# Weights as fp32 over the hardware rings with casts on chip, shared taps and diagonals, and half rows of x, in a fused convolution and GELU block

## The chip, the cores and the metric

The kernel runs on one core of one Trainium2 chip. Its matrix products run on TensorE (PE in the profiles); VectorE (DVE), ScalarE (ACT) and GpSimd (POOL) do the element-wise work; SyncE (SP) only issues transfers here. A "ring" is the queue of transfers of an engine. The metric is the device time of one execution in microseconds (us); lower is better. Each kernel was run several times beside the kernel before on the same chip. Beside each run stands the mean clock that TensorE was granted (1.00 is full speed).

## The reference, cut to what matters

```python
w = softmax(weight, axis=-1)                 # 8 heads x 7 taps
x_pad = concat([zeros(B, 6, 192), x], 1)     # causal, 8 x 4096 x 192
y[b, s, ch] = sum_k w[head(ch), k] * x_pad[b, s + k, ch]     # head(ch) = ch // 24
h = y.reshape(32768, 192) @ w_in             # 192 x 2048
out = gelu(h) @ w_out                        # 2048 x 192, fp32 out
```

All inputs and the output are fp32 in memory; the two matrix products run in bf16.

## The kernel before

The 32768 tokens are cut into two halves that run side by side in partitions 0 to 63 and 64 to 127, and each half into blocks: six of 256 tokens, then blocks of 512. Blocks 0 and 1 are convolved by TensorE with diagonal matrices (the taps), the later ones by VectorE. Per block TensorE does the first product in slices, ScalarE applies gelu to each slice, and TensorE does the second product of the block before between the slices.

The weights come over GpSimd's queue, whose DMAs cast fp32 to bf16 on the way. Half of `win` is loaded, and VectorE copies each piece across to the other 64 partitions (`dup`):

```python
for i in range(3):                      # GpSimd
    win_in(FP[i], FP[i + 1], S_WIN[i])  # win (bf16) <- moe_w_in (fp32), two halves
halo(0)
g.dma_start(ap(wout, ...), ap(woutt, ...)).then_inc(S_WOUT, 16)   # patterns cut
# ... cut ...
v.tensor_scalar(wnm[0:H, 0:KS], wex[:, :], wrc[:, 0:1], None, ALU.mult)   # VectorE: softmax,
v.transpose(wnt[:, :], wnm[:, :])       # then a column of taps per channel, by transposes
for q in range(4):
    v.transpose(ap(wcol, 32 * q * NP * 32, ...), ap(wch, DQ * (q % 2), ...))
diag(0); diag(1)                        # diagonals of two thirds; ScalarE makes the third's
for p in range(NP): trans(0, p)         # x of block 0, in whole rows: 32x32 transposes
dup(0)
conv_out(v, 0, 1); conv_out(v, 0, 4)    # convolved block 0 out of PSUM
dup(1); dup(2)
for p in range(NP): trans(1, p)
for p in range(NP): cast(1, p)
for j in range(len(PIECES)): conv_out(v, 1, j)
# ... cut: then transposes and convolution of block 2 and on ...
t.wait_ge(S_WARM, 1)                    # TensorE
for i in range(16):
    t.matmul(hp[1][:, 0:512], warm[:, 0:128], warm[:, :])   # warm-ups on zeros
```

In block 0, gelu groups 0 to 7 need the weight slices in pairs: groups 0 and 1 need slice 0, groups 4 and 5 need slice 2. The second product of block 0 is spread over block 1's eight groups as 3, 4, 4, 4, 4, 4, 4, 4 parts of 31 (6 units of 64 in the first).

## Time and profile before

| | before |
|---|---|
| median of three runs | 683.74 us (683.59 to 684.27) |
| span of the profiled run | 682.0 us |
| first tap on TensorE | 7.51 us |
| first gelu | 10.59 us |
| first second-product matmul | 19.24 us |
| first first-product matmul of block 2 | 29.76 us |

The last four lines are read from the instructions in order of time and from the chain of work that ended last. They are the marks by which kernels are compared: once the second product has begun, TensorE hardly waits any more, so whatever is lost or won up to there is carried to the end.

### The profile page before, as it was taken

The page shows a single profiled execution, that of the slowest core. Times are in us where ns is not written, and L with a number is a line of the kernel's source. Part 1 is how long each engine was busy: PE and PEld are TensorE (multiplying, and loading weights), DVE is VectorE, ACT ScalarE, POOL GpSimd, SP SyncE. Part 2 cuts the span into 40 slices and gives each one's busy share as a digit, 9 for nine tenths or more (in the row PEclk, how much of TensorE's full clock was granted, in tenths as well). Part 3 has the DMA queues.
Part 4 walks back from the last instruction along what each step waited for, and adds up shares of the span by engine and source line. Part 5 has one row for each costly group of instructions (what it writes and reads, how often), then busy time and mean ns, then how long its engine had stood idle before and what let it go on. Part 6 is the DMA issues. An engine that isn't in the chain of part 4 may idle for free.

```text
span 682.0 us, 27319 instructions
## 1 busy us (share of the span) xinstructions
PE 676.2 (99%) x12576; PEld 407.5 (60%) x12576; DVE 562.2 (82%) x909; ACT 538.4 (79%) x557; POOL 35.1 (5%) x51
## 2 busy tenths in 40 slices
PE   8999999999999999999999999999999999999998
PEld 4899655555555555555555555555555555555556
DVE  7899979888889888899888898888898888988611
ACT  7899988777787777787777788777778777778772
POOL 4026100000000000000000000000000000000000
PEclk9999999999999999999999999999999999999999
DMA  9345322134432143332234322334422434310223
GB/s 178 77 107 130 83 60 72 44 78 95 95 94 54 45 94 94 95 77 52 63 94 95 94 68 45 80 94 96 94 53 46 95 94 96 82 43 21 48 49 94
DMA packets 132946, 54.00 MB, mean 79 GB/s; under 512 B 126432, under 2 KB 132704, under 8 KB 132832
## 3 DMA queue, kind: packets, MB, share of 16 engines
q1 hardware_dynamic: 129872, 49.93, 31.5%
q0 software_dynamic: 2288, 1.57, 1.6%
q8 instruction: 98, 1.61, 1.0%
q10 hardware_dynamic: 672, 0.76, 0.4%
q14 instruction: 16, 0.13, 0.1%
HBM read 28.66 MB, written 25.17 MB: 79 GB/s over the span
## 4 chain that ended last, share of the span: by engine, by line
PE 97%; ACT 2%; issue 0%; DVE 0%
PE hp L774 47%; PE ob L838 43%; PE ob L805 6%; ACT gT L694 2%; PE hp L708 1%; PE ob L727 0%; ACT xc L192 0%; ACT osb L261 0%; DVE osb L303 0%; DVE osb L272 0%; DVE warm L452 0%
## 5 line engine op out<-in xcount | busy, mean ns | idle before, releaser
L694 ACT ACTIVATE gT<-hp 128x1024 bf16<-128x1024 f32 x512 | 522.8, 1023 | 129.3 <-PE hp L774 126.0
L774 PE MATMUL hp<-xc,win 64*64 64x512 bf16 (+2 forms) x6048 | 418.9, 366 | 1.5 <-ACT gT L694 0.7
L838 PE MATMUL ob<-gT,wout 64*64 64x512 bf16 x5376 | 366.3, 376 | 0.0
L561 DVE SCALAR_TENSOR_TENSOR acc<-xT,wcol,acc 128x512 f32<-128x512 f32 (+1 forms) x495 | 314.6, 700 | 0.5 <-ACT acc L667 0.5
L774 PEld LDWEIGHTS hp<-xc,win 64*64 64x64 bf16 (+1 forms) x6048 | 187.7, 106 | 136.3 <-ACT gT L694 2.5
L838 PEld LDWEIGHTS ob<-gT,wout 64*64 64x64 bf16 x5376 | 172.2, 118 | 122.9
L303 DVE STREAM_TRANSPOSE osb<-ob 128x512 f32<-128x512 f32 x84 | 74.2, 886 | 100.8 <-PE ob L838 100.8
L528 DVE STREAM_TRANSPOSE xT<-xin 128x512 f32<-128x512 f32 (+1 forms) x105 | 78.7, 803 | 2.1 <-DMA xin<-in_x_dram 2.1
L561 DVE SCALAR_TENSOR_TENSOR xc<-xT,wcol,acc 128x512 bf16<-128x512 f32 (+1 forms) x99 | 65.3, 717 | 0.0
L438 POOL COPY xT<-xT 128x18 f32<-128x18 f32 x30 | 27.9, 930 | 515.3 <-DVE xT L528 492.3
L805 PE MATMUL ob<-wout,gT 64*128 64x192 bf16 x1024 | 52.2, 243 | 0.3
L805 PEld LDWEIGHTS ob<-wout,gT 64*128 64x128 bf16 x1024 | 43.5, 94 | 6.4 <-PE ob L805 0.6
L554 DVE TENSOR_SCALAR acc<-xT,wcol 128x512 f32<-128x512 f32 (+1 forms) x90 | 37.6, 474 | 1.1
L274 ACT ACTIVATE osb<-ob 128x192 f32<-128x192 f32 x4 | 1.3, 330 | 9.5 <-PE ob L805 9.5
L272 DVE COPY osb<-ob 128x192 f32<-128x192 f32 x4 | 1.4, 357 | 8.4 <-PE ob L805 8.4
L708 PE MATMUL hp<-warm 128*128 128x512 bf16 x16 | 6.3, 581 | 1.3 <-DVE warm L452 1.3
L261 ACT ACTIVATE osb<-ob 128x384 f32<-128x384 f32 x12 | 5.8, 487 | 0.0
L667 ACT ACTIVATE acc<-xT,wcol 128x256 f32<-128x256 f32 (+1 forms) x9 | 5.2, 575 | 0.0
L708 PEld LDWEIGHTS hp<-warm 128*128 128x128 bf16 x16 | 2.1, 139 | 4.9 <-issue 3.6
L194 DVE CAST xc<-ob 64x256 bf16<-64x256 f32 (+3 forms) x8 | 2.8, 358 | 1.6 <-PE ob L727 1.4
L376 POOL DMA_DIRECT2D win<-in_moe_w_in_dram x6 | 3.9, 653 | 0.0
L497 DVE COPY win<-win 64x768 bf16<-64x768 bf16 (+1 forms) x6 | 3.1, 509 | 0.2
(33 smaller groups left out, 21.7 us busy)
## 6 DMA issues: line engine op xcount, KB each, us to landing
out_dram<-osb SPq DMA_DIRECT2D x122, 192.0 KB, 3.1
xin<-in_x_dram SPq DMA_DIRECT2D x116, 192.0 KB, 4.1
xin<-in_x_dram SPq DMA_DIRECT2D x20, 96.0 KB, 3.2
wout<-in_moe_w_out_dram POOLq DMA_DIRECT2D x1, 768.0 KB, 11.0
win<-in_moe_w_in_dram POOLq DMA_DIRECT2D x4, 96.0 KB, 4.2
win<-in_moe_w_in_dram POOLq DMA_DIRECT2D x2, 192.0 KB, 4.8
out_dram<-osb SPq DMA_DIRECT2D x8, 48.0 KB, 1.7
out_dram<-osb ACTq DMA_DIRECT2D x4, 96.0 KB, 1.9
```

Of the source, the lines that this page charges most:

```text
L261: e.activation(out=dst, in_=src, func=AF.Copy).then_inc(S_EVA)
L303: v.transpose(ap(osb[m % 2], j, [[8 * C, 128], [C // 2, TB // 32], [NP, 32]]), bank(ring(m, j)),).then_inc(S_EV)
L438: g.tensor_copy(dst, src).then_inc(S_HALO)
L528: v.transpose(ap(xT[n % 2], p * XW + HX, [[NP * XW, 128], [1, w]]), ap(xin[n % NX], p, [[TB // 32 * DQ, 128], [D if n == 0 else DQ, w // 3 ...
L554: ins = v.tensor_scalar(a, src, wk, None, ALU.mult)
L561: ins = v.scalar_tensor_tensor(dst, src, wk, a, op0=ALU.mult, op1=ALU.add)
L667: a.activation(out=acc[n % 2][:, p * TB : p * TB + w], in_=ap(xT[n % 2], p * XW + HX, [[NP * XW, 128], [1, w]]), func=AF.Copy, scale=wcol[ ...
L694: a.activation(out=ap(gT[n % 2], i * c * 2 * w, dst), in_=ap(hp[u % 2], 0, src), func=AF.Gelu,).then_inc(S_GELU)
L708: t.matmul(hp[1][:, 0:512], warm[:, 0:128], warm[:, :])
L774: ins = t.matmul(hp[u % 2][fo : fo + fw, o : o + w], ap(win, f1, [[NP * F, 64], [2, fw]]), xc[n % 2][r, p * TB : p * TB + w], start=(p == ...
L805: ins = t.matmul(bank(bb[sub], w=C), gT[m % 2][r, c0 : c0 + 128], wout[r, CH[i] * C : (CH[i] + 1) * C], start=(ph == 0 and i == 0), stop=( ...
L838: ins = t.matmul(bank(ring(m, j), slice(64 * h, 64 * h + 64), w), ap(wout, 64 * hf * NF * C + CH[i] * C + j, [[NF * C, 64], [NP, 64]],), g ...
```

## The change

The intent is a shorter start: take the weights off GpSimd's slower queue, shorten the chain that makes the taps, load less of x first, and spread the casts over two engines. The whole weights are now loaded as fp32 by SyncE and ScalarE and cast by VectorE and GpSimd: `own` casts a piece of `win` where it landed, `dup` casts it across to the other half of the partitions, and `wcast` casts a piece of `wout`. The diff, cut to its core:

```diff
-        wcol = sbt("wcol", [128, NP * 32], F32)
-        dg = sbt("dg", [128, NP * KS * 64], BF16)
+        wcol = sbt("wcol", [128, KS], F32)
+        winf = sbt("winf", [128, NP * F // 2], F32)
+        woutf = sbt("woutf", [128, NF * C], F32)
+        dg = sbt("dg", [128, KS * 64], BF16)
 ... GpSimd
+            g.dma_start(wsb[:, :], ap(wt, 0, [[KS, H], [0, 64 // H], [1, KS]])).then_inc(S_WSB, 16)
 ...
-            for i in range(3):
-                win_in(FP[i], FP[i + 1], S_WIN[i])
             halo(0)
-            g.dma_start(ap(wout, ...), ap(woutt, ...)).then_inc(S_WOUT, 16)
+            own(g, OWNG[0]).then_inc(S_OWN)          # cast of weight slice 1
             halo(1)
+            for p in range(NP):
+                cast(1, p)                           # block 1's x to bf16
+            own(g, OWNG[1]).then_inc(S_OWN)          # cast of weight slice 3
+            for i in range(2):
+                wcast(g, i).then_inc(S_WOG)          # half of wout
 ... VectorE
-            diag(0)
-            diag(1)
             for p in range(NP):
                 trans(0, p)
-            dup(0)
+            own(v, 0).then_inc(S_DUPE)               # cast of weight slice 0
+            dup(0, 0)                                # reads winf (fp32), writes win (bf16)
             conv_out(v, 0, 1)
             conv_out(v, 0, 4)
-            dup(1)
-            dup(2)
+            dup(0, 1)
+            dup(1, 0)
+            dup(1, 1)
             for p in range(NP):
                 trans(1, p)
-            for p in range(NP):
-                cast(1, p)
+            own(v, 2).then_inc(S_DUPE)
+            for s in (2, 3):
+                for hf in range(2):
+                    dup(s, hf)
             for j in range(len(PIECES)):
                 conv_out(v, 1, j)
+            for i in range(2, 4):
+                wcast(v, i).then_inc(S_WOC)          # the other half of wout
 ... ScalarE
             load(a, 0, (2, 3))
             a.wait_ge(S_PRO, 1)
             a.activation(out=wex[:, :], in_=wsb[:, :], func=AF.Exp, ...)
+            for s in range(2):
+                win_in(a, s, 1)
 ... TensorE
-            share = {1: [3, 4, 4, 4, 4, 4, 4, 4]}
 ... SyncE
-            sp.dma_start(wsb[:, :], ap(wt, 0, [[KS, H], [1, KS]])).then_inc(S_WSB, 16)
             load(sp, 0, (0, 1))
-            sp.wait_ge(S_WIN[0], 32)
+            for s in range(2):
+                win_in(sp, s, 0)
             load(sp, 1)
+            for s in range(2, 4):
+                for hf in range(2):
+                    win_in(sp, s, hf)
+            for i in range(4):
+                wout_in(sp, i)
             load(sp, 2)
```

More of the change, by code (lines that the diff above doesn't have):

```diff
@@ L112, in bass_lightweight_conv__then__act_gelu_exact_kernel @@
         wout = sbt("wout", [128, NF * C], BF16)
-        wsb = sbt("wsb", [H, KS], F32)
-        wmx = sbt("wmx", [H, 1], F32)
-        wsm = sbt("wsm", [H, 1], F32)
-        wrc = sbt("wrc", [H, 1], F32)
-        wex = sbt("wex", [H, KS], F32)
-        wnm = sbt("wnm", [32, 32], F32)
-        wnt = sbt("wnt", [32, 32], F32)
-        wch = sbt("wch", [32, D], F32)
-        wcol = sbt("wcol", [128, NP * 32], F32)
+        wsb = sbt("wsb", [64, KS], F32)
+        wmx = sbt("wmx", [64, 1], F32)
+        wsm = sbt("wsm", [64, 1], F32)
+        wrc = sbt("wrc", [64, 1], F32)
+        wex = sbt("wex", [64, KS], F32)
+        wcol = sbt("wcol", [128, KS], F32)
+        winf = sbt("winf", [128, NP * F // 2], F32)
+        woutf = sbt("woutf", [128, NF * C], F32)
         idb = sbt("idb", [128, 64], BF16)
-        dg = sbt("dg", [128, NP * KS * 64], BF16)
+        dg = sbt("dg", [128, KS * 64], BF16)
         warm = sbt("warm", [128, 512], BF16)
@@ L136, in bass_lightweight_conv__then__act_gelu_exact_kernel @@
         S_WSB = sem("S_WSB")
-        S_WIN = [sem("S_WIN%d" % i) for i in range(3)]
-        S_WOUT = sem("S_WOUT")
+        S_WIN = [sem("S_WIN%d" % i) for i in range(4)]
+        S_WOUT = [sem("S_WOUT%d" % i) for i in range(4)]
         S_XIN = [sem("S_XIN%d" % i) for i in range(NX)]
@@ L151, in bass_lightweight_conv__then__act_gelu_exact_kernel @@
         S_PCA = sem("S_PCA")
-        S_DGA = sem("S_DGA")
         S_DUPE = sem("S_DUPE")
+        S_OWN = sem("S_OWN")
+        S_WOC = sem("S_WOC")
+        S_WOG = sem("S_WOG")
         S_HALO = sem("S_HALO")
@@ L203, in wait_pc, with cast, own, wcast @@
                 e.wait_ge(S_PCE, 2 + (1, 3, 6)[p])
+        def cast(e, n, p):
+            e.wait_ge(S_TR, NP * n + p + 1)
+            e.tensor_copy(
+                ap(xTb[PC[n]], p * XB + HX, [[NP * XB, 128], [1, WS[n]]]),
+                ap(xT[n % 2], p * XW + HX, [[NP * XW, 128], [1, WS[n]]]),
+            ).then_inc(S_CAST[PC[n]])
         NCV = NP * KS
-        FQ = F // 8
         FH = F // 2
-        FP = [0, FQ, 2 * FQ, FH]
+        FP = [0, 256, 512, 768, FH]
+        OWNV = (0, 2)
+        OWNG = (1, 3)
+        WG = [0, 4, 2, 6]
+        def own(e, s):
+            e.wait_ge(S_WIN[s], 32)
+            return e.tensor_copy(
+                ap(win, FP[s], [[NP * F, 128], [F, NP], [1, FP[s + 1] - FP[s]]]),
+                ap(winf, FP[s], [[NP * FH, 128], [FH, NP], [1, FP[s + 1] - FP[s]]]),
+            )
+        def wcast(e, i):
+            e.wait_ge(S_WOUT[i], 16)
+            o = 2 * WG[i] * C
+            return e.tensor_copy(wout[:, o : o + 4 * C], woutf[:, o : o + 4 * C])
+        def win_in(e, s, hf):
+            e.dma_start(
+                ap(winf, 64 * hf * NP * FH + FP[s], [[NP * FH, 64], [FH, NP], [1, FP[s + 1] - FP[s]]]),
+                ap(wint, hf * FH + FP[s], [[NP * F, 64], [F, NP], [1, FP[s + 1] - FP[s]]]),
+            ).then_inc(S_WIN[s], 16)
+        def wout_in(e, i):
+            g = WG[i]
+            e.dma_start(
+                ap(woutf, 2 * g * C, [[NF * C, 128], [2 * C, 2], [1, 2 * C]]),
+                ap(woutt, 256 * g * C, [[2 * C, 128], [256 * C, 2], [1, 2 * C]]),
+            ).then_inc(S_WOUT[i], 16)
         def cvd(n):
@@ L313, in load @@
                 off = ((q // 2) * HALF + OFF[n]) * D + DQ * (q % 2)
+                dst = [[TB // 32 * DQ, 32], [DQ, mb], [1, DQ]]
                 if n == 0:
-                    dst = [[TB // 32 * DQ, 32], [1, mb * D - DQ]]
-                    src = [[mb * D, 32], [1, mb * D - DQ]]
+                    src = [[mb * D, 32], [D, mb], [1, DQ]]
                 else:
-                    dst = [[TB // 32 * DQ, 32], [DQ, mb], [1, DQ]]
                     src = [[D, 32], [32 * D, mb], [1, DQ]]
@@ L373, in _ @@
         def _(g):
-            def win_in(c0, c1, sm):
-                for hf in range(2):
-                    g.dma_start(
-                        ap(win, 64 * hf * NP * F + c0, [[NP * F, 64], [F, NP], [1, c1 - c0]]),
-                        ap(wint, hf * FH + c0, [[NP * F, 64], [F, NP], [1, c1 - c0]]),
-                    ).then_inc(sm, 16)
+            g.dma_start(
+                wsb[:, :], ap(wt, 0, [[KS, H], [0, 64 // H], [1, KS]])
+            ).then_inc(S_WSB, 16)
             g.wait_ge(S_MSET, 1)
@@ L441, in _ @@
             halo(0)
-            g.dma_start(
-                ap(wout, 0, [[NF * C, 128], [2 * C, NF // 2], [1, 2 * C]]),
-                ap(woutt, 0, [[2 * C, 128], [256 * C, NF // 2], [1, 2 * C]]),
-            ).then_inc(S_WOUT, 16)
+            own(g, OWNG[0]).then_inc(S_OWN)
             halo(1)
+            for p in range(NP):
+                cast(g, 1, p)
+            own(g, OWNG[1]).then_inc(S_OWN)
+            for i in range(2):
+                wcast(g, i).then_inc(S_WOG)
             for n in range(2, NB):
@@ L453, in _ @@
             v.memset(idb[:, :], 1.0).then_inc(S_MSET)
-            v.memset(wnm[:, :], 0.0).then_inc(S_MSET)
             v.wait_ge(S_WSB, 16)
@@ L463, in _ @@
             v.wait_ge(S_PRO, 3)
-            v.wait_ge(S_MSET, 2)
-            v.tensor_scalar(
-                wnm[0:H, 0:KS], wex[:, :], wrc[:, 0:1], None, ALU.mult
-            ).then_inc(S_PRO)
-            v.wait_ge(S_PRO, 4)
-            v.transpose(wnt[:, :], wnm[:, :]).then_inc(S_PRO)
-            v.wait_ge(S_PRO, 5)
-            v.tensor_copy(
-                ap(wch, 0, [[D, 32], [GRP, H], [1, GRP]]),
-                ap(wnt, 0, [[32, 32], [1, H], [0, GRP]]),
-            ).then_inc(S_PRO)
@@ L476, in _ @@
-            v.wait_ge(S_PRO, 6)
-            for q in range(4):
-                v.transpose(
-                    ap(wcol, 32 * q * NP * 32, [[NP * 32, 32], [1, NP * 32]]),
-                    ap(wch, DQ * (q % 2), [[D, 32], [1, NP], [NP, 32]]),
-                ).then_inc(S_PRO)
-            v.wait_ge(S_PRO, 10)
-            v.wait_ge(S_IDN, 2)
-            def diag(p):
-                v.tensor_tensor(
-                    ap(dg, p * KS * 64, [[NP * KS * 64, 128], [64, KS], [1, 64]]),
-                    ap(idb, 0, [[64, 128], [0, KS], [1, 64]]),
-                    ap(wcol, p * 32, [[NP * 32, 128], [1, KS], [0, 64]]),
-                    ALU.mult,
-                ).then_inc(S_DG)
@@ L493, in dup @@
-            def dup(s):
-                v.wait_ge(S_WIN[s], 32)
-                for hf in range(2):
-                    v.tensor_copy(
-                        ap(
-                            win,
-                            64 * (1 - hf) * NP * F + FH + FP[s],
-                            [[NP * F, 64], [F, NP], [1, FP[s + 1] - FP[s]]],
-                        ),
-                        ap(
-                            win,
-                            64 * hf * NP * F + FP[s],
-                            [[NP * F, 64], [F, NP], [1, FP[s + 1] - FP[s]]],
-                        ),
-                    ).then_inc(S_DUPE)
@@ L510, in cast @@
-            def cast(n, p):
-                v.wait_ge(S_TR, NP * n + p + 1)
-                v.tensor_copy(
-                    ap(xTb[PC[n]], p * XB + HX, [[NP * XB, 128], [1, WS[n]]]),
-                    ap(xT[n % 2], p * XW + HX, [[NP * XW, 128], [1, WS[n]]]),
-                ).then_inc(S_CAST[PC[n]])
+            for hf in range(2):
+                v.tensor_scalar(
+                    wcol[64 * hf : 64 * hf + 64, :], wex[:, :], wrc[:, 0:1], None, ALU.mult
+                ).then_inc(S_PRO)
@@ new lines, in _, with dup @@
+            v.wait_ge(S_PRO, 5)
+            v.wait_ge(S_IDN, 2)
+            v.tensor_tensor(
+                ap(dg, 0, [[KS * 64, 128], [64, KS], [1, 64]]),
+                ap(idb, 0, [[64, 128], [0, KS], [1, 64]]),
+                ap(wcol, 0, [[KS, 128], [1, KS], [0, 64]]),
+                ALU.mult,
+            ).then_inc(S_DG)
+            def dup(s, hf):
+                v.wait_ge(S_WIN[s], 32)
+                v.tensor_copy(
+                    ap(
+                        win,
+                        64 * (1 - hf) * NP * F + FH + FP[s],
+                        [[NP * F, 64], [F, NP], [1, FP[s + 1] - FP[s]]],
+                    ),
+                    ap(
+                        winf,
+                        64 * hf * NP * FH + FP[s],
+                        [[NP * FH, 64], [FH, NP], [1, FP[s + 1] - FP[s]]],
+                    ),
+                ).then_inc(S_DUPE)
@@ L532, in trans @@
                         p,
-                        [[TB // 32 * DQ, 128], [D if n == 0 else DQ, w // 32], [NP, 32]],
+                        [[TB // 32 * DQ, 128], [DQ, w // 32], [NP, 32]],
                     ),
@@ L550, in conv @@
                 src = ap(xT[n % 2], p * XW + HF + kt, [[NP * XW, 128], [1, w]])
-                wk = wcol[:, p * 32 + kt : p * 32 + kt + 1]
+                wk = wcol[:, kt : kt + 1]
                 a = acc[n % 2][:, p * TB : p * TB + w]
@@ L616, in _ @@
         def _(a):
-            a.wait_ge(S_WARM, 1)
-            a.activation(out=hot[:, 0:1], in_=warm[0:1, 0:1], func=AF.Exp).then_inc(S_ACTP)
+            a.activation(
+                out=hot[:, 0:1], in_=nc.const_aps.tensor(0.0, (1, 1), F32), func=AF.Exp
+            ).then_inc(S_ACTP)
             load(a, 0, (2, 3))
@@ L628, in _ @@
             ).then_inc(S_ACTP)
-            a.activation(out=hot[:, 1:2], in_=warm[0:1, 0:1], func=AF.Gelu).then_inc(S_HOT)
-            a.wait_ge(S_PRO, 10)
-            a.wait_ge(S_IDN, 2)
-            for k in range(KS):
-                d0 = ((NP - 1) * KS + k) * 64
-                c0 = (NP - 1) * 32 + k
-                a.activation(
-                    out=dg[:, d0 : d0 + 64],
-                    in_=idb[:, :],
-                    func=AF.Copy,
-                    scale=wcol[:, c0 : c0 + 1],
-                ).then_inc(S_DGA)
+            a.activation(
+                out=hot[:, 1:2], in_=nc.const_aps.tensor(0.0, (1, 1), F32), func=AF.Gelu
+            ).then_inc(S_HOT)
+            for s in range(2):
+                win_in(a, s, 1)
+            a.wait_ge(S_PRO, 5)
             for p in range(NP):
@@ L670, in first_tap @@
                     func=AF.Copy,
-                    scale=wcol[:, p * 32 + KS - 1 : p * 32 + KS],
+                    scale=wcol[:, KS - 1 : KS],
                 ).then_inc(S_K0)
@@ L715, in pconv @@
                     if n == 0:
-                        if p < NP - 1:
-                            t.wait_ge(S_DG, p + 1)
-                        else:
-                            t.wait_ge(S_DGA, KS)
+                        t.wait_ge(S_DG, 1)
                 if k == KS - 2:
@@ L724, in pconv @@
                     r = slice(64 * hf, 64 * hf + 64)
-                    d0 = (p * KS + k) * 64
+                    d0 = k * 64
                     x0 = p * XB + (32 * k if n == 0 else HF + k) + c0
@@ L759, in mm1 @@
                         t.wait_ge(S_CV, cvd(n))
-                if n == 0 and i in (0, 2, 4):
-                    t.wait_ge(S_WIN[i // 2], 32)
-                    t.wait_ge(S_DUPE, 2 * (i // 2) + 2)
+                if n == 0:
+                    t.wait_ge(S_DUPE, (2, 3, 4, 5, 7, 8, 9, 10)[i])
+                    t.wait_ge(S_OWN, sum(s <= i // 2 for s in OWNG))
                 for cc in range(c):
@@ L869, in _ @@
                     new = M0 < n <= M1
-                    ws = SHARE if new else share.get(n, [1] * NSL[n])
+                    ws = SHARE if new else [1] * NSL[n]
                     a0 = len(todo) * sum(ws[:i]) // sum(ws)
                     a1 = len(todo) * sum(ws[: i + 1]) // sum(ws)
-                    if n == 1 and a0 == 0 and a1 > 0:
-                        t.wait_ge(S_WOUT, 16)
+                    if n == 1 and i < 2:
+                        t.wait_ge((S_WOG, S_WOC)[i], 2)
                     for un in todo[a0:a1]:
@@ L885, in _ @@
         def _(sp):
-            sp.dma_start(wsb[:, :], ap(wt, 0, [[KS, H], [1, KS]])).then_inc(S_WSB, 16)
             load(sp, 0, (0, 1))
-            sp.wait_ge(S_WIN[0], 32)
+            for s in range(2):
+                win_in(sp, s, 0)
             load(sp, 1)
+            for s in range(2, 4):
+                for hf in range(2):
+                    win_in(sp, s, hf)
+            for i in range(4):
+                wout_in(sp, i)
             load(sp, 2)
-            sp.wait_ge(S_WOUT, 16)
             load(sp, 3)
```

## The prediction

> **What bounds the kernel now.** I read the page's busy table and its chain of work that ended last, then the same chain for the first 20 us, then the start in order of time, and last the waits, because the change touches only the start.
>
> ```profile
> PE 676.2 (99%) x12576; PEld 407.5 (60%) x12576; DVE 562.2 (82%) x909; ACT 538.4 (79%) x557; POOL 35.1 (5%) x51
> PE 97%; ACT 2%; issue 0%; DVE 0%
> ```
>
> TensorE holds 97% of the chain. Every byte of weights and both prologue blocks are over by about 20 us, so the other 660 us cannot change except by being shifted. What counts is the moment at which TensorE begins its unbroken run. The chain of the first 20 us, piece by piece (start, length, what):
>
> ```profile
> 1.26 6.32 PE hp L708 x16
> 7.58 0.90 PE ob L727 x22
> 8.50 0.38 ACT xc L192
> ...
> 9.94 0.63 PE hp L774 x8
> 10.59 1.94 ACT gT L694 x2
> ...
> 13.62 0.83 PE hp L774 x12
> 14.45 0.89 PE ob L727 x28
> ...
> 18.51 0.83 PE hp L774 x12
> 19.34 0.58 PE ob L805 x12
> ```
>
> L708 is the 16 warm-up matmuls, L727 the convolution taps of blocks 0 and 1, L192 the ScalarE copies of the convolved block, L774 the first matmul, L694 gelu, L805 the second matmul. The reader is to see that the chain does not pass through the x load, the softmax of the taps or the diagonals. It passes through the warm-ups, which end at 7.58, and the taps follow at once. From 10.59 to about 18.5 it alternates between gelu and TensorE; from 18.51 it is TensorE without a gap.
>
> The same stretch in order of time (start, us, engine, line), and then its waits (who waited for whom: us in total, times, longest):
>
> ```profile
> 6.36 1.34 DVE L528 STREAM_TRANSPOSE xT<-xin 128x256 f32<-128x256 f32 x3
> ...
> 7.51 1.63 PE L727 MATMUL ob<-xTb,dg 64*64 64x256 bf16 x56
> ...
> 19.39 1.34 DVE L528 STREAM_TRANSPOSE xT<-xin 128x256 f32<-128x256 f32 x3 [1.72 <-DMA xin<-in_x_dram]
> ```
>
> ```profile
> PEld ob L727 <- ACT xTb L643: 0.4, 1, 0.4
> ...
> PEld ob L727 <- DVE xTb L512: 0.2, 1, 0.2
> ...
> PEld ob L805 <- DMA wout<-in_moe_w_out_dram: 0.2, 1, 0.2
> ```
>
> The first two lines show that TensorE takes its first tap at 7.51, before the modelled end of the last warm-up, and that the transposes of block 0 start at 6.36, after the diagonals. The third of them is block 2's transposes, which waited 1.72 us for x. The waits are of weight loads that stood ready 0.4, 0.2 and 0.2 us early; the matmuls in front of them covered most of that. So the waits that the change can remove are small.
>
> **What the Trainium skill says.** "TensorE: Matmul & The Clock Gate", Part 1, says that an idle array runs at half rate until a window of activity has passed, with 426.7 ns between 512-column matmuls. This trace agrees: the warm-up weight loads stand 0.43 us apart (1.66, 2.09, ... 5.93, 6.36), tighter only at the last ones. "DMA: Bandwidth & Descriptors", SWDGE vs HWDGE vs iDMA, says that only DMAs issued by GpSimd can cast; so fp32 over the hardware rings needs casts on the engines. The trace fits: both weights are issued by POOL. "VectorE: DVE Perf Modes", The perf-mode tier table, gives an fp32 copy in SBUF the two-fold rate; here the cast of 128x256 fp32 to bf16 took 285 ns, less than the 350 ns of the one-pass scaling of the same shape and less than the 424 ns out of PSUM. "SBUF — State Buffer", SBUF: two separate sides, says that VectorE in such a mode and GpSimd shut each other out of a shared port pair. The trace shows something of that kind: POOL's 18-element copy took about 300 ns in the first 34 us and 1001 ns after, beside a busy VectorE.
>
> **The change, part by part.**
>
> *Taps and diagonals.* Before, from the landing of the weights of the taps at 2.16: wcol is ready at 5.28, the two diagonals at 6.44, ScalarE's seven at 7.06. Now one scaling, one copy, five transposes and one of the two 0.62 us diagonals go. From the landing to the reciprocal's end is 3.16 - 2.16 = 1.0 us; two scalings add about 0.4, one diagonal 0.62: 2.1 us from landing with the gaps. The landing moves to the POOL ring, whose first DMAs need about 0.65 us of issue; I estimate 2.8 to 3.2. So the diagonals are ready near 5.1, 1.3 us earlier.
>
> *x of block 0.* The four loads shrink from 180 to 96 KB. Before, they were issued from 1.25 on and the last landed at about 1.7 + 4.6 = 6.3 (issue to landing by issue). Now they start at about 0.8; 393 KB at the 225 GB/s that the x queue made in the first 34 us is 1.75 us, so they land near 4.2. Transposes can start at about 5.1 instead of 6.36, and ScalarE's first cast would let TensorE start at 5.1 + (7.51 - 6.36) = 6.25.
>
> *But TensorE is not free at 6.25.* The warm-ups stay sixteen and start on the same VectorE memset. The durations (mean 581 ns, some 610 at half rate and 380 at full) make the last one start at about 7.2 and stream until about 7.4. So the first tap moves from 7.51 to about 7.4: **0.1 us of the 1.26 us gained**. With all casts and halos ready, the taps no longer pace behind them, which I put at another 0.1. After that the four ScalarE copies (1.38 us) and the first matmul are unchanged. First gelu: 10.59 becomes about 10.4.
>
> *Casts of win.* By 285 ns for 256 columns and 0.52 ns for each further one (two per cycle), a piece of 768 takes about 0.55 us on VectorE. Before block 2 it gains 2 own casts, 2 wout casts and 8 copies across halves, 12 x 0.55 = 6.6 us, and loses 0.87 + 2.31 = 3.2 of the old copies and 0.67 of casts of block 1. The room is there: it now starts 1.3 us earlier, and it waited 0.39 and 1.72 us for x and 1.25 for TensorE. My timetable: first own and cross copy done at 7.6 to 8.1 (mm1 starts at 9.2), pieces of slice 1 at 10.4, x of block 1 transposed at 11.75, last cross copy at 14.5; slice 2 is wanted at about 13.4 and its first copy is there at 12.9. It fits with 0.5 us to spare at the tightest.
>
> *Casts on POOL.* From 128x186 in 379 ns and 128x18 in 218, about 0.96 ns per column: 0.45 us for 256 and 0.94 for 768. Own piece done by about 8.5 (wanted at 11), block 1's casts by 12.5 (taps at 14.2; before, they came 0.2 late from VectorE, so up to 0.1 is gained), second own piece by 15.5 (wanted at 16.5), wout by 17.5 to 18 (wanted at 18.9; before it came 0.2 late, so another 0.1).
>
> *Transfers.* The software queue took 31.9% of 34 us, 10.8 us of all engines. The same weights are 3.15 MB as fp32; at an estimated 290 GB/s (between the 225 of the 384-byte packets and the 302 of the first x loads) that is again 10.8 us. x falls by 0.35 MB. So x of block 2 lands at about 18.6 instead of 19.4. VectorE is then done with wout at about 18.6. Its convolution takes 28.77 - 19.39 = 9.4 us, so it is ready at 28.0, against a first matmul of block 2 at 29.76: no stall.
>
> *Sum on the path:* 0.2 (taps) + up to 0.1 (block 1's taps) + up to 0.1 (wout) = 0.2 to 0.4 us; I take 0.25 and round: 683.74 - 0.25 = 683.5. The split of the second matmul over block 1's slices (8 units in the first slice for 6) changes order, not work.
>
> **Rivals.** (a) *The earlier prologue counts in full*: the first tap comes 1.3 us earlier and the total is 682.4. For it: x, softmax and diagonals do end that much earlier. Against it: warm-ups run up to the first tap in the chain, with no gap, and the change leaves them. (b) *A new wait takes the place*: POOL is shut out by VectorE's fp32 copies back to back from 11.8 to 14.5 and casts block 1 or wout late, or block 2's x lands later than 20.4 behind 3.15 MB on the same ring. For it: the 1001 ns copies, and a slack of only about 1 us at block 2's convolution. Each would cost 0.5 to 1.5 us once: 684.2 to 685.2. (c) *ScalarE*: it issues two win pieces before its casts; if these issue only after the gelu table load, the first piece lands at 8 and the first matmul loses 0.2: 683.7.
>
> **Range and chances.** I give rival (a) one in ten, rival (b) one in five, the rest to 683.2 to 683.8, where the three runs of before alone spread over 0.7. So 682.6 to 684.8. Two per cent would be 13.7 us, more than the whole stretch between the first tap and the second matmul; only a mistake in the order of waits could cost that, and nothing here could gain it.
>
> **What would show it.** Right: the chain of the first 20 us again starts with the warm-ups until about 7.5 and goes straight to the taps; the taps' weight loads wait for the warm-ups and no longer for ScalarE; diagonals end near 5.1 and transposes of block 0 start near 5.1; first gelu at 10.3 to 10.5; first second-matmul at 18.8 to 19.2. Wrong: warm-ups that end earlier; a wait of TensorE on POOL's casts or on VectorE's copies of win above 0.3 us; block 2's first matmul waiting for the convolution, with transposes of block 2 starting after 20.4.

## The result

| | before | changed |
|---|---|---|
| runs | 683.59 to 684.27 | 686.27, 686.76, 687.31, 687.29 |
| median | 683.82 us | **687.02 us** |
| mean granted clock of the runs | (profiled run) 1.00 | 0.997 to 0.998 |
| first tap | 7.51 | 7.33 |
| first gelu | 10.59 | 12.31 |
| first second-product matmul | 19.24 | 22.28 |
| block 2's first matmul | 29.76 | 32.31 |
| span of the profiled run | 682.0 | 684.6 |

The ratio is 1.0044, with a 95% interval of 1.0027 to 1.0062. Ratios here are the mean time of one kernel's fast runs over that of the other's of the same rounds, so not quite the ratio of the medians. The change costs 3 us, which is within 2% but outside the predicted range of 682.6 to 684.8.

The page of the changed kernel, busy times and the chain by engine:

```profile
PE 675.7 (99%) x12576; PEld 408.9 (60%) x12576; DVE 564.1 (82%) x905; ACT 537.2 (78%) x550; POOL 35.9 (5%) x52
...
PE 96%; ACT 2%; DMA 1%; issue 1%; DVE 0%; POOL 0%; ACTq 0%; POOLq 0%
```

TensorE's work is the same as before, but a DMA now stands in the chain with 1%. The chain of the first 24 us of the changed kernel, in order of time (start, length, what):

```profile
1.32 2.80 DMA wsb<-in_weight_dram
...
4.40 0.30 ACT wex L637
...
5.13 4.99 DMA winf<-in_moe_w_in_dram
...
11.09 3.78 PE hp L781 x35
...
14.89 1.03 ACT gT L703
15.93 0.80 issue
16.73 0.83 PE hp L781 x12
17.56 0.89 PE ob L733 x28
...
21.61 0.83 PE hp L781 x12
22.44 0.66 PE ob L812 x16
```

The warm-ups have left the chain. In their place stand the load of the taps' weights, the exponential behind it, and a piece of `winf` that was issued after the exponential. Then the gelu groups run, there is a hole of 0.80 before the fifth one (16.73), and the second product begins at 22.44 instead of 19.34. The same stretch on VectorE, in order of time:

```profile
9.13 0.69 DVE L226 CAST win<-winf 128x768 bf16<-128x768 f32 x1 [1.55 <-DMA winf<-in_moe_w_in_dram]
9.85 0.68 DVE L514 CAST win<-winf 64x768 bf16<-64x768 f32 x1
10.57 0.63 DVE L195 CAST xc<-ob 64x256 bf16<-64x256 f32 x2
11.23 2.12 DVE L514 CAST win<-winf 64x768 bf16<-64x768 f32 x3
13.38 1.35 DVE L538 STREAM_TRANSPOSE xT<-xin 128x256 f32<-128x256 f32 x3
14.64 0.68 DVE L226 CAST win<-winf 128x768 bf16<-128x768 f32 x1
15.35 3.92 DVE L514 CAST win<-winf 64x768 bf16<-64x768 f32 x4
```

VectorE stood idle 1.55 us for the weight piece, and the convolved block's copy (L195), which was ready to be made long before, stood behind the two casts in the same queue. TensorE's first group starts at 11.09 because that copy ended at about 11.0. The chain names GpSimd's cast of slice 1 there, which ended at the same time; by the code group 0 waits for no cast of GpSimd, and the trace of experiment e3 names VectorE's copy at that place. The four copies from 15.35 on took 3.92 us, where four alone would take 2.7.

TensorE's granted clock, by the view of busy time in stretches (stretch, length, PE, PEld, DVE, ACT, POOL busy, then PE's clock, DMA share, GB/s):

```profile
11.00:12.00 1.00, 0.91 (x12) 0.63 (x14) 0.94 (x3) 0.00 (x0) 0.15 (x1) 0.75 1.12 239
12.00:13.00 1.00, 1.00 (x14) 0.90 (x12) 0.97 (x2) 0.69 (x1) 0.00 (x0) 0.50 1.12 249
...
14.00:15.00 1.00, 1.00 (x12) 0.56 (x10) 1.00 (x3) 0.72 (x2) 0.98 (x3) 0.54 1.06 372
```

After about 2 us without a matmul (from 9.0 to 11.1) the array ran at half its clock for 3 us. In the kernel before the same column reads 1.00 throughout the start, also during the warm-ups, whose weight loads stand 0.43 us apart at first and closer at the end; so it does not show every slow stretch.

On TensorE's side the two traces give this sum up to the fifth group: 12.31 - 10.59 = 1.72 us for the late first gelu; from there to the end of the third gelu 3.61 us (15.92 - 12.31) instead of 2.98 (13.57 - 10.59), 0.63 more, with the half clock; then a hole of 0.80. The sum is 3.15; the fifth group came 16.73 - 13.62 = 3.11 later.

This is a sum and not yet a cause. The fifth group waits for VectorE's first copy of slice 2, and VectorE works without a gap from the landing at 9.13 to the end of that copy (15.35 + 1.27 = 16.62). At full clock TensorE would have come 0.63 us sooner and waited that much longer: the half clock is hidden behind VectorE here, and f1 below bears this out. On VectorE's side, set against e1 below (weight piece at 7.77, this copy 0.69 long, fifth group at 14.78), the 3.11 are 1.36 for the late piece, 0.58 for the longer copy and 1.16 that e1 still has against the kernel before (14.78 - 13.62), in which VectorE has less to do before that point.

Up to block 2 about 0.55 came back: from the first second-product matmul in the chain to block 2's first slice 32.31 - 22.44 = 9.87 us instead of 29.76 - 19.34 = 10.42.

### The profile page after: what moved, and what is told of

It is laid out like the page before. It is cut to its first block, busy times and chain, and to the rows that moved or that the text cites. A ratio compares the mean times of both kernels' runs of the same rounds, so it can differ in the third digit from the quotient of the medians.

```text
span 684.6 us, 27324 instructions
## 1 busy us (share of the span) xinstructions
PE 675.7 (99%) x12576; PEld 408.9 (60%) x12576; DVE 564.1 (82%) x905; ACT 537.2 (78%) x550; POOL 35.9 (5%) x52
## 4 chain that ended last, share of the span: by engine, by line
PE 96%; ACT 2%; DMA 1%; issue 1%; DVE 0%; POOL 0%; ACTq 0%; POOLq 0%
PE hp L781 48%; PE ob L843 42%; PE ob L812 5%; ACT gT L703 2%; DMA winf<-in_moe_w_in_dram 1%; DMA wsb<-in_weight_dram 0%; PE ob L733 0%; ACT osb L301 0%; DVE osb L343 0%; POOL win L226 0%; DVE osb L312 0%; ACT L644 0%; ACT wex L637 0%; DVE wmx L490 0%; ACTq L238 0%
## 5 line engine op out<-in xcount | busy, mean ns | idle before, releaser
L514 DVE CAST win<-winf 64x768 bf16<-64x768 f32 x8 | 6.6, 820 | 0.3
L733 PE MATMUL ob<-xTb,dg 64*64 64x256 bf16 (+1 forms) x112 | 3.2, 245 | 0.8 <-ACT xTb L652 0.8
L733 PEld LDWEIGHTS ob<-xTb,dg 64*64 64x64 bf16 x112 | 2.6, 106 | 1.7 <-ACT xTb L652 1.3
```

Source lines behind the costliest of these rows:

```text
L514: v.tensor_copy(ap(win, 64 * (1 - hf) * NP * F + FH + FP[s], [[NP * F, 64], [F, NP], [1, FP[s + 1] - FP[s]]],), ap(winf, 64 * hf * NP * FH ...
L733: ins = t.matmul(bank(kd, slice(64 * ho, 64 * ho + 64), w), dg[r, d0 : d0 + 64], xTb[PC[n]][r, x0 : x0 + w], start=(k == KS - 1), stop=(k ...
```

## The experiments

Theory: the loss is made of (1) the order of issue, in which ScalarE's weight pieces stand behind an exponential that waits for the taps' weights; (2) VectorE's longer casts and copies, partly beside GpSimd's; (3) more bytes on the rings. Rivals were that the volume alone sets everything, that the other two parts of the change cost or gain, and later that the clock does. Each kernel was run five or six times beside the kernel before, whose medians were 683.93, 683.96, 683.62 and 683.87.

### e1: ScalarE's weight pieces issued early

```diff
             load(a, 0, (2, 3))
+            for s in range(2):
+                win_in(a, s, 1)
             a.wait_ge(S_ACTP, 1)
 ...
-            for s in range(2):
-                win_in(a, s, 1)
```

> The changed kernel with ScalarE issuing its two pieces of the first matmul's weights right after its two x loads, before the exponential, instead of behind it. Theory (issue order): the pieces were issued at 4.50 and 5.13 only because ScalarE's queue stood behind the exponential, which waits for the taps' weights (landed at 4.13); issued at about 2.5 and 3.1 and with the 4.2 us to landing of the other half they land near 6.7 to 7.3, VectorE's first cast starts right after the transposes (7.6 instead of 9.13), first gelu at 10.2 to 10.6 instead of 12.31, no half-clock stretch at 12 to 14. Slice 2's copy on VectorE is then still late by 1 to 1.6, so the whole gains about 1.5: 685.3 to 685.8. Rival (volume): the fp32 weights and x fill the 16 engines whatever the order, so the first piece still lands near 9 and the time stays within 0.4 of 687.

Measured: 686.24 (685.36 to 686.60), ratio 1.0030 (1.0016 to 1.0043); all five runs at clock 1.00. First gelu 10.68, second product from 20.59. The front came back as the issue-order theory had it, 1.6 us of the 1.72, and the half clock was gone. But the median fell only by 0.8. TensorE's waits and VectorE's transposes of block 2 in this run say where the rest went:

```profile
PE hp L781 <- ACT gT L703: 2.1, 3, 1.3
PE hp L781 <- DVE xc L571: 1.5, 1, 1.5
```

```profile
22.73 0.93 DVE L538 STREAM_TRANSPOSE xT<-xin 128x256 f32<-128x256 f32 x2 [0.74 <-DMA xin<-in_x_dram]
```

TensorE now waits 1.5 us for block 2's convolution, whose x came at 22.7 instead of 19.4. That second bound was hidden behind the first in the changed kernel. By the traces it takes back all that the front won: block 2 starts at 32.25 here and at 32.31 in the changed kernel, whose profiled run, its fastest, took 686.27, as long as e1's median. What the 0.8 between the medians is, the clock perhaps, is not shown. The first wait's longest part, 1.3, stands before the fifth group, which waits for gelu and for VectorE's copy of slice 2; gelu had long been done.

### e2: the taps' weights on SyncE

```diff
-            g.dma_start(wsb[:, :], ...).then_inc(S_WSB, 16)
 ...
         def _(sp):
+            sp.dma_start(wsb[:, :], ap(wt, 0, [[KS, H], [0, 64 // H], [1, KS]])).then_inc(S_WSB, 16)
             load(sp, 0, (0, 1))
```

> The changed kernel with the taps' weights loaded at the head of SyncE's queue (same 64-partition pattern) instead of by GpSimd. Theory (issue order): they land near 2.2 instead of 4.13, ScalarE's exponential and so its two weight pieces come about 1.9 earlier (issue near 2.6), diagonals end near 4.2; TensorE's first tap moves only to the end of the warm-ups; first gelu near 10.0 to 10.5, second-matmul start about 1.5 to 2.2 earlier than 22.3; time 684.8 to 685.5. Rival (volume): the same landing near 9 as before, within 0.4 of 687. Rival (prologue counts): below 684.

Measured: 687.42, a miss. The marks moved in the expected direction (transposes of block 0 at 5.43, first tap 6.56, first gelu 10.62, second product 20.56), though the taps' weights landed at 3.33 and not near 2.2, and the wait for block 2's convolution is there again with 1.5 us. The one run at clock 1.00, which is also the profiled one, took 686.28, as much as e1; the four at 0.997 to 0.998 took 687.31 to 687.57. It also shows that an earlier first tap by itself is worth nothing here: the tap came 0.95 before that of the kernel before, and the first gelu did not.

### e3: GpSimd keeps out of VectorE's way

```diff
+            g.wait_ge(S_DUPE, 7)
             own(g, OWNG[1]).then_inc(S_OWN)
```

> The changed kernel with GpSimd waiting, before its second cast of the first matmul's weights, until VectorE has copied slice 2's first half across (7 of its copies), so the two never cast side by side there. Theory (contention): that VectorE copy took 1.27 us instead of 0.69 beside GpSimd's cast, so slice 2 of block 0 starts about 0.6 earlier (16.1 instead of 16.73) and the whole gains 0.4 to 0.6: 686.4 to 686.6. Rival (VectorE is late by its own order of work, contention or not): within 0.2 of 687, and the copy still ends near 16.6.

Measured: 686.56 (686.32 to 686.68), ratio 1.0038 (1.0025 to 1.0050), which overlaps the changed kernel's interval, so the time does not settle it. Nor does the clock: its runs at 1.00 took 686.32 and 686.59, those at 0.997 to 0.998 took 686.56 to 686.68. The trace does. VectorE's first two copies of slice 2 across:

```profile
16.16 1.41 DVE L515 CAST win<-winf 64x768 bf16<-64x768 f32 x2
```

They took 1.41 us instead of 2.23 for the same two in the changed kernel, and the hole before the fifth group shrank from 0.80 to 0.18. Of that, 0.25 is this run's own: the first gelu came 1.06 later here (13.37, as its weight piece landed at 9.9), the copies started only 0.81 later. Contention is a real but small term.

### b1, b2, b3: the other parts alone, on the kernel before

b1 is the shared taps and diagonals (64-partition load on SyncE, one `wcol`, one `dg`), b2 the half rows of x (the change's edits of `load` and `trans`), b3 both.

```diff
 b2, b3:
-                    dst = [[TB // 32 * DQ, 32], [1, mb * D - DQ]]
-                    src = [[mb * D, 32], [1, mb * D - DQ]]
+                    dst = [[TB // 32 * DQ, 32], [DQ, mb], [1, DQ]]
+                    src = [[mb * D, 32], [D, mb], [1, DQ]]
```

> The kernel before with the two other parts alone: one set of taps and diagonals (their weights loaded on SyncE into 64 partitions) and block 0's x in half rows; weights still cast by GpSimd's DMAs, 16 warm-ups. Theory (warm-ups bound the start): diagonals end near 4.3 and transposes start near 5 instead of 6.36, yet TensorE's first tap moves only to the end of the warm-ups, 7.4 at most 0.1 to 0.3 earlier than 7.51; time 683.3 to 683.8 against 683.8. Rival (these parts count in full): first tap 1.0 to 1.3 earlier, 682.5 to 682.8. Rival (these parts themselves cost): above 684.3.

> The kernel before with one set of taps and diagonals alone (weights of the taps on SyncE into 64 partitions; x of block 0 in whole rows, weights by GpSimd). b3, with the half rows too, gave 684.41 against 683.93, its taps' weights landing at 3.49 instead of 2.16 and block 0's x still at 6.6. Theory (start bound by x's landing and by the warm-ups): diagonals end near 5.7 instead of 6.4, transposes start at 6.2 to 6.6, nothing gained or lost: 683.7 to 684.3. Rival (shorter chain counts): 683.0 or less.

> The kernel before with block 0's x in half rows alone. Theory: half the bytes in four times the packets (384 instead of 5760 bytes each) land no earlier beside GpSimd's weights, so the transposes still start at the diagonals' end, 6.36 to 6.5: 683.7 to 684.3. Rival (half the bytes, earlier landing and room for the weights): 683.4 or less; rival (half rows cost): 684.5 or more.

Measured: b3 684.41, b1 684.27, b2 684.27, with ratios 1.0005, 1.0005 and 1.0006, all intervals around 1. Neither part gains and neither can be shown to cost. The transposes of block 0 in b3:

```profile
5.09 0.62 DVE L463 TENSOR_TENSOR dg<-idb,wcol 128x448 bf16<-128x448 bf16 x1
6.61 1.34 DVE L505 STREAM_TRANSPOSE xT<-xin 128x256 f32<-128x256 f32 x3 [0.90 <-DMA xin<-in_x_dram]
```

The diagonals end at 5.7, but half the bytes of x in short packets landed at 6.6, no earlier than the whole rows in the kernel before, whose transposes began at 6.36. In b1 and b2 the transposes began at 6.98 and 7.06; in b2, which keeps the old taps, the diagonals had ended only 0.2 before. So beside GpSimd's weight loads, once the taps' chain is shorter, the start is held by x. Here the prediction's reason was incomplete: it named the warm-ups, which in b3 had ended at 6.2 by the order of time.

### e6: x of block 2 before the second product's weights

On e1:

```diff
+            load(sp, 2)
             for i in range(4):
                 wout_in(sp, i)
-            load(sp, 2)
```

> e1 (ScalarE's weight pieces issued early) with block 2's x issued before, not after, the four loads of the second matmul's weights on SyncE. In e1 the first gelu came back to 10.68 and the second matmul started at 20.6 instead of 22.3, but TensorE then waited about 1.5 us for block 2's convolution, whose x landed at 22.7 behind 3.15 MB of fp32 weights, against 19.4 in the kernel before. Theory (the ring's bytes are the second bound): x of block 2 now lands near 18 to 19 and that wait goes, but the weights land 1 to 1.5 later (last near 22.5), so TensorE waits 0.5 to 1.5 for them instead at the second slice of block 1: 685.5 to 686.3, about what e1 had (686.24). Rival (only the order was wrong): no new wait, 684.6 to 685.0.

Measured: 686.52 (685.88 to 686.66), ratio 1.0036. TensorE's waits:

```profile
PE ob L812 <- DVE wout L235: 1.5, 1, 1.5
PE hp L781 <- DVE xc L571: 0.6, 1, 0.6
```

The wait changed its place: 1.5 us now for the casts of `wout`, whose pieces landed last, and 0.6 for the convolution still, because its transposes stand behind those casts on VectorE. The Trainium skill says the same of the queues: "DMA: Bandwidth & Descriptors", Issuing engines are not separate DMA queues, has them all end on the same 16 DMA engines. Order alone did not help here.

### e7: the second product's weights over GpSimd's casting DMA again

On e1: no `wout_in`, no `wcast`; after `halo(0)` GpSimd issues the kernel before's `wout` DMA, and TensorE waits for that.

> e1 with the second matmul's weights cast by GpSimd's DMA into bf16 again, as in the kernel before, and no casts of them on chip; the first matmul's weights stay fp32 with casts. Theory (the ring's bytes are the second bound): the ring carries 1.57 MB less, block 2's x lands near 19 to 20 instead of 22.7, the 1.5 us wait for its convolution goes; the weights land near 19 to 20, the second matmul starts at 20.5 as in e1: 684.5 to 685.1. Rival (the 16 engines were equally busy either way, the software queue takes as long): x of block 2 still near 22 and 685.8 to 686.3.

Measured: 684.69 (684.24 to 684.81), ratio 1.0009 (0.9997 to 1.0022): e1 and e7 together bring back 2.3 of the 3.2 us. e7 takes away four casts of `wout` on VectorE and GpSimd too, not only bytes from the rings; but in e1 block 2's transposes had waited for x itself (0.74 us), and that is what goes. VectorE's transposes of block 2 in this run:

```profile
19.81 1.35 DVE L540 STREAM_TRANSPOSE xT<-xin 128x256 f32<-128x256 f32 x3
```

They start at 19.81 with no wait for x, and the wait of TensorE for the convolution is gone. The rival (the 16 engines are as busy either way) falls. It was also the prediction's own estimate. The rings' rates in e1 and, by contrast, here, in the view of stretches:

```profile
10.00:14.00 4.00, 3.09 (x47) 1.82 (x44) 3.88 (x8) 3.31 (x4) 1.66 (x4) 1.00 1.12 225
14.00:18.00 4.00, 3.22 (x86) 2.47 (x88) 3.87 (x5) 2.29 (x3) 1.97 (x3) 1.00 1.08 355
18.00:22.50 4.50, 3.97 (x74) 2.86 (x72) 3.04 (x8) 3.68 (x5) 0.79 (x2) 1.00 1.08 175
```

```profile
18.00:22.50 4.50, 4.05 (x88) 3.36 (x78) 4.31 (x13) 3.94 (x5) 0.32 (x1) 1.00 0.81 175
```

The last two columns are the DMA share, which may pass 1, and GB/s. In e1 the engines are full until 22.5. In e7 they have room in the last stretch. This stretch reads 0.28 in the kernel before.

### e8: copies across from the bf16 result

On e7: `dup` reads `win` in bf16, after waiting for the cast that made it, instead of `winf`.

> e7 (684.69: second matmul's weights cast by GpSimd's DMA, first matmul's weights fp32 with casts) with VectorE's eight copies across the halves reading the bf16 result of the casts, as in the kernel before (0.42 us each), instead of the fp32 piece (0.69 to 1.27 us). Theory (VectorE's own work is the last front bound): slice 2 of block 0, which waited 1.3 us in e7 for its copy, waits 0.2 to 0.5; second matmul starts near 19.8 instead of 20.7; 683.7 to 684.1. Rival (slice 2 waits for its piece to land or for the casts, not for the copies): 684.5 to 684.8.

Measured: 684.25 against 683.62, ratio 1.0009 (0.9996 to 1.0021), so the time is not told from e7's. The trace of the tile `win` gives the copies' lengths (least, median, longest ns), e7 and then e8:

```profile
L516 DVE CAST win<-winf x8: 685/687/934, 8.7 to 16.8; 64x768 bf16<-64x768 f32 x8
```

```profile
L519 DVE COPY win<-win x8: 418/420/884, 8.5 to 15.6; 64x768 bf16<-64x768 bf16 x8
```

A copy takes 420 instead of 687 ns, and the longest wait of TensorE on the gelu line falls from 1.3 to 0.5, as in the kernel before. So the hole before the fifth group was VectorE's copies. TensorE then waits 0.6 for `wout`'s DMA.

### e9: longer runs for the weights

On e1: slices 2 and 3 of `winf` in two transfers with runs of 2 KB instead of four with 1 KB.

> e1 (686.24) with the second half of the first matmul's fp32 weights loaded in two transfers with runs of 2 KB instead of four with runs of 1 KB. In e1 the rings moved 225 GB/s while these weights and x came and 355 while the second matmul's weights (runs of 1.5 KB) came. Theory (short runs set the rate of the first stretch): x of block 2 lands 0.5 to 1 earlier than 22.7, the wait for its convolution shrinks from 1.5 to 0.5 to 1: 685.3 to 685.8. Rival (rate independent of the run's length; slice 2's weights also land later, since two slices share a semaphore): 686.2 or more.

Measured: 686.05, ratio 1.0039. Three runs at clock 1.00 took 685.61 to 686.05; two at 0.995 and 0.998 took 688.52 and 688.12. The profiled run is a slow one: the merged pieces landed at 14.8, TensorE stood idle 3.3 us for slice 2, and its clock was about 0.50 from 15.5 to 22. Between 12 and 14 us the rings moved 205 GB/s. Longer runs did not raise the rate; why it is 225 in the first stretch and 355 in the next stays open. One rival stands untested: by the code `winf` goes to 64 partitions and `woutf` to 128, and e9 changed the length of the runs but not the partitions. Loads of x mixed in do not explain it: in e1 only 61 of the 860 packets between 10 and 14 us were shorter than 512 bytes, so nearly all were `winf`.

### c1 and c2: what the change does right, on the kernel before

c1 is one line, the even spread of block 0's second product:

```diff
-                    ws = SHARE if new else share.get(n, [1] * NSL[n])
+                    ws = SHARE if new else [1] * NSL[n]
```

c2 adds b1's taps and ScalarE's first activation from a constant.

> The kernel before with the one scheduling part of the change alone: block 0's second matmul is spread evenly over the eight slices of block 1 (8 units each) instead of 6 in the first and more in the others. Theory (the groups of 16 units then end with the slices): in the changed kernel TensorE went from its first second-matmul at 22.44 to block 2's first slice at 32.31, 9.87 us, against 10.42 in the kernel before (19.34 to 29.76), where it waited twice 0.3 for itself within the slices; so 0.3 to 0.5 faster: 683.4 to 683.7 against 683.95. Rival (order only, as the prediction had it): 683.8 to 684.1.

> c1 plus the shared taps and diagonals and ScalarE's first activation from a constant (so that its x loads issue at 0.9 instead of 1.25); weights by GpSimd, x in whole rows. Theory: x of block 0 lands up to 0.3 earlier and the diagonals no longer hold the transposes, which start at 6.0 to 6.3; TensorE's warm-ups end at 6.6 to 7.6, so at most 0.2 more than c1: 683.2 to 683.6. Rival (x of block 0 lands at 6.4 to 7 anyway, as in b1 with 684.27): 683.6 to 683.9, no better than c1.

Measured: c1 683.51 and c2 683.54 against 683.62, ratios 0.9998 (0.9985 to 1.0010) and 1.0000. In c1's trace TensorE takes 29.92 - 20.06 = 9.86 us from its first second-product matmul to block 2, against 10.42 before, and the two waits of 0.3 on itself are gone. The theory's 0.55 us is there in the trace; the profiled run lost most of it again further up: VectorE waited 1.46 us for the third piece of `win`, and block 1's transposes, which stand behind its copies, came at 13.34 instead of 12.20. At five runs the gain in time is not shown, so no version here is shown to beat the kernel before.

### f1 and f2: matmuls in the idle gap

```diff
             for kd in order:
                 pconv(*seq[kd].pop(0))
+            for i in range(8):                      # f2: on e2, 6
+                t.matmul(hp[1][:, 0:512], warm[:, 0:128], warm[:, :])
```

> The changed kernel with eight 512-column matmuls of zeros after the taps of block 0, which fill the 2 us in which TensorE stood idle (9.0 to 11.1) before its granted clock fell to 0.50 from 11.5 to 14.5. Theory (the idle gap itself costs, by the clock): the granted clock stays 1.00, slices 0 to 3 of block 0 go as fast as before (3.03 us from first gelu to the third gelu's end instead of 3.60), but slice 2's copies are still late, so the second matmul starts 0 to 0.6 earlier; the runs lose their spread to 687.3 and lie at 686.0 to 686.5. Rival (the clock's fall is hidden behind VectorE's late copies): within 0.2 of 687.0 with the same spread.

> e2 (taps' weights on SyncE) with six such matmuls after the taps. In e2 TensorE took its taps at 6.56 and then stood idle 1.5 us before the first slice; its profiled run (686.3, clock 1.00) was the fast one, the other four lay at 687.3 to 687.6. Theory (the slow runs are those in which the clock fell in that gap): all runs now lie near 686.0 to 686.4. Rival (the slow runs have another cause): still mostly near 687.4.

Measured: f1 688.45 (688.07 to 689.12), slower than the changed kernel: a clear miss. The first gap's half clock did go (clock 1.00 from 6 to 18 us). The clock then fell at the next gap, the wait for slice 2, where dense work follows. Busy time in two stretches of f1, before and after that point:

```profile
16.00:17.00 1.00, 0.00 (x0) 0.00 (x0) 0.97 (x2) 0.79 (x1) 1.00 (x3) 1.00 1.12 384
...
20.00:21.00 1.00, 1.00 (x12) 0.57 (x8) 0.94 (x3) 0.00 (x0) 0.00 (x0) 0.50 1.31 227
```

Block 1's taps and the groups between them then ran at half speed (the first taps 1.43 us instead of 0.96). f1's first gelu was also later, 12.90, since the first piece landed at 10.03 in this run, 0.90 later than in the changed kernel. The fifth group came 0.93 later (17.66 for 16.73), as VectorE's first copy of slice 2 did, although the half clock before it was gone: the hole grew instead. So f1's rival was right on this stretch (the clock's fall is hidden behind VectorE's late copies), though not on the time. From the fifth group to the second product f1 and f2 take 7.06 us, the changed kernel 5.55 (22.28 - 16.73) and e2's profiled run 5.55: at that place the half clock costs 1.5 us. The call's runs of the kernel before hold one at 687.1 with clock 0.998, the only such; without it f1's ratio would be a little higher. f2: 686.87, with three runs at clock 1.00 at 686.29, 686.53 and 686.49, and three at 0.998 at 687.33, 687.48 and 687.22. So filling one gap did not stop the fall. In f2 and e2 the two groups of times are exactly the two clocks; in e3 they are not, and the changed kernel's four runs lie 1.0 us apart at one clock. A run's mean clock alone does not tell its time.

## Why the prediction was wrong

**What held.** The time stayed within 2%, and nothing after the first 30 us changed but by being shifted. A faster chain of the taps, and half rows of x, are worth nothing by themselves (b1, b2, b3; e2's early tap). Rival (b), a new wait in the old one's place, is what came, and its kinds were named: late x of block 2 behind 3.15 MB on one ring, and GpSimd against VectorE. The second came the other way round: not GpSimd was shut out, VectorE's copy was lengthened. (The sign given for it, POOL copies of 1001 ns after 34 us, misreads a mean: of the 27 copies the median is 447 ns, and two of 3.6 and 11.9 us make most of the rest.) Luck: the first tap, predicted at 7.4, came at 7.33, but for other reasons. The diagonals and transposes, predicted for 5.1, ended and began at about 6.3, the warm-ups ended at 6.56 and not at 7.4, and TensorE waited 0.77 us for ScalarE's cast of x.

**"First own and cross copy done at 7.6 to 8.1."** This step failed first, and it is the largest. The copy was done at 10.5. The taps' weights landed at 4.13, not at 2.8 to 3.2; ScalarE's two weight pieces stood behind the exponential that waits for them, were issued at 4.50 and 5.13 and needed 4.6 and 5.0 us to land. Rival (c) had this order but let it cost 0.2, from "lands at 8"; it cost 1.72 up to the first gelu, since two casts of 0.69 follow and the convolved block's copy stands behind them. e1 undid the order alone and got 1.6 back.

**"A piece of 768 takes about 0.55 us on VectorE."** That fits a piece of `wout`, one run per partition (558 ns for 128x768). A piece of `win`, three runs of 256, took 0.69, and up to 1.27 beside a cast of GpSimd. By the predicted timetable slice 2's first copy was there at 12.9 "with 0.5 us to spare"; it came at about 16.6. The mechanism was right, the term was mis-sized: with the late front it made the fifth group late, and in e1, with the front mended, a wait of 1.3. e3 and e8 shortened the copies and with them the wait.

**"3.15 MB at an estimated 290 GB/s ... again 10.8 us."** In e1 all queues together made 225 GB/s while almost only `winf` came (10 to 14 us) and 355 only from 14 to 18, with `woutf`. x of block 2 landed at 22.7 in e1, not at 18.6. The changed kernel hides this, because its front is later still; e1 and e6 show it as 1.5 us of wait, and e7 takes it away.

**What the prediction did not have.** TensorE's clock falls in the idle gap that the late piece makes. In the changed kernel's trace it stretches the first groups by 0.63 us, which VectorE's late copy hides; where it falls at the next gap, in f1, it costs 1.5. Between the two groups of runs in e2 and f2 lies 1.0 us. And the even spread "changes order, not work" was wrong as a reason for no effect: it took 0.55 us off block 1 in the changed kernel's trace and in c1's.

What stays open: why the first stretch's DMA rate is low (the number of partitions was not tested), and how much of the changed kernel's time is clock, since all its four runs had the lower one.

## What to carry to other kernels

Before moving a load to another queue, write down what stands in front of it in that queue, and what those instructions wait for: a DMA behind a wait is issued when the wait ends, however early its data is wanted. Casting on chip trades a slow casting DMA for the whole fp32 volume on the rings and for engine time on the path; check both against the next consumer of the ring, not only against the first. And mend one bound before judging the next: here the second (x of block 2) showed as no wait of TensorE until the first was gone. The same goes for sums: a stretch that got slower is a loss only if nothing else holds the next step, so follow the wait that ends last, here VectorE's.

## What the Trainium skill lacked or had wrong

- "TensorE: Matmul & The Clock Gate", HAM oscillation, how this bites in real kernels, gives as its rule no idle gap above about 3.4 us. Here the granted clock fell to 0.50 after gaps of about 2 us (9.0 to 11.1 in the changed kernel, 15.7 to 17.7 in f1), while e2's profiled run, with gaps of 1.5 and 1.4 us, stayed at 1.00. For these gaps the rule is too generous.
- "SBUF — State Buffer", SBUF: two separate sides, explains the lock but has no figure for a pair of casts: VectorE's copy went from 0.69 to 1.27 beside one of GpSimd's casts of 0.82.
- No page has what spreading a tiny load over partitions costs: the taps' weights landed 1.35 and 1.56 us after issue in 8 rows (the kernel before, b2), and 2.5, 2.7 and 2.9 in 64 rows on the same queue (e2, b3, b1), beside loads of x.
